# A bit field of the weight decode moves to a PSUM bank, and short-lived results share two banks instead of three

## The chip, the cores and the metric

The kernel runs on one core of a Trainium2 chip. The core has five engines that run side by side: TensorE (PE in the profile; PEld is its loading of stationary weights), VectorE (DVE), ScalarE (ACT), GpSimd (POOL) and SyncE (SP), which only issues transfers here. Results of TensorE land in PSUM[...]; everything else lives in SBUF. The metric is the device time of one execution in microseconds (us). The kernel before took 1086.1 us (median of three runs, 1086.04 to 1087.46).

## What is computed

Two blocks follow each other: an attention in which a query sees only the keys of its own cluster, and a feed-forward block with a hard-swish gate.

```python
# B, H, S, D = 4, 8, 768, 64; 16 clusters per head
q_assign = argmax(normalised(q) @ normalised(centroids))      # per head
k_assign = argmax(normalised(k) @ normalised(centroids))
mask   = q_assign[:, :, :, None] == k_assign[:, :, None, :]
scores = where(mask, q @ k.T / 8, -1e9)
attn   = softmax(scores) @ v                                   # (B, H, S, D)
x = attn.transpose(0, 2, 1, 3).reshape(3072, 512)
h = x @ w_in                                                   # w_in: 512 x 2048
y = (h * clip(h + 3, 0, 6) / 6) @ w_out                        # w_out: 2048 x 512
```

The weights `w_in` and `w_out` arrive as 64-bit floats. [...]the kernel takes each weight as two 32-bit words (`lo`, `hi`) and builds the 32-bit float from them: this is the *decode*, in 32 chunks of 128 x 512 weights.

## The kernel before

The work goes in rounds of two score tiles (`n`, `n + 1`); twelve tiles make a pair of heads, 48 a batch. The decode is spread over the first two batches (`n` = 0 to 94), so that it lies beside the attention. From `n` = 54 on the feed-forward block of the first batch (`ph`) is mixed in as well.

PSUM's eight banks are used like this: scores `ps` four (two tiles of two banks), `pv` one, the pool `psum_t` one, the pool `psum_m` two.

```python
psum_s = pool("psum_s", 2, space=PSUM)
psum_v = pool("psum_v", 1, space=PSUM)
psum_t = pool("psum_t", 1, space=PSUM)
psum_m = pool("psum_m", 2, space=PSUM)
...
st = {"scratch": 0}

def scratch(shape, name):          # the short-lived results pqk, pcs, pr, po, pd
    st["scratch"] += 1
    if st["early"] and st["scratch"] % 3:
        return psum_m.tile(shape, F32, name=name, tag="m")
    return psum_t.tile(shape, F32, name=name, tag="t")
```

While `st["early"]` holds, that is until the decode ends, two of three short-lived results go to `psum_m` and one to `psum_t`. The feed-forward results `ph` and `py` always go to `psum_m`.

The decode of a chunk is five steps; three to five of them (once one) are emitted at the end of each round:

```python
def split():
    load_weights(i + 1)                       # transfer of the next chunk, two buffers
    raw = st.pop(("raw", i))
    got.update(lo=raw[:, :, 0], hi=raw[:, :, 1])
    got["size"] = decp.tile([P, WC], BF16, name="wsize")
    got["top"]  = decp.tile([P, WC], U32, name="wtop")      # SBUF
    got["unit"] = decp.tile([P, WC], U32, name="wunit")     # SBUF
    nc.scalar.activation(out=got["size"], in_=hi, func=ACT.Abs, ...)
    nc.vector.tensor_scalar(out=top, in0=hi, ...)           # L219: hi << 3, masked
def join():
    nc.vector.scalar_tensor_tensor(out=top, in0=hi, in1=top, ...)   # L225
def power():
    nc.scalar.activation(out=got["size"], in_=got["size"], func=ACT.Relu, ...)
    nc.vector.tensor_scalar(out=unit, in0=top, ...)         # L235: & 0xFF800000
def rest():
    nc.vector.scalar_tensor_tensor(out=unit, in0=lo, in1=unit, ...) # L241
def total():
    nc.vector.tensor_tensor(out=weight, in0=top, in1=unit, op=ALU.add)  # L246
# (arguments cut)
```

The parts of the attention that matter here, per round and in the order in which they are emitted:

```python
scores(n)        # PE: ps <- xf (L371), += xm (L371); ACT: ex = exp(ps) (L383);
                 # POOL: acc += ex (L387, L390)
attn_v(n - 2)    # PE: pv += v * ex (L400)
later            # ACT: range sums of the last rcp (L433, L434), or counts
divide           # every third round: PE: pd <- ones, acc (L421);
                 # DVE: rcp = 1 / pd (L425), xT = num * rcp (L426)
prep of the next pair, by place r of the round in its pair:
  r = 0, 2: turn: PE: pqk (L295), ACT: xf <- pqk (L297), twice per round
  r = 4: PE: pcs (L308), ACT: cs <- pcs (L313)
  r = 6: PE: pr (L319), DVE: mx, one_hot <- pr (L322, L328)
  r = 8: route_turn twice, r = 10: once: PE: po (L351), ACT: xm <- po (L355)
feed-forward: PE: ph (L457), ACT and DVE: g_sb <- ph (L444, L445)
decode steps: share = {0: 5, 2: 3, 4: 4, 6: 1, 8: 3, 10: 4}
```

`divide` falls on the rounds with r = 2 and r = 8, so a `pd` is always followed by two `pqk` or two `po` (with a `ph` ahead of the first one in some rounds).

Of the kernel before, what the change touches and what calls it, by code (L numbers as in the profile page):

```python
# [10 lines left out]
U32 = mybir.dt.uint32  # L11
# [7 lines left out]
P = 128  # L19
# [10 lines left out]
WC = 512  # L30
# [86 lines left out]
def fast_path(ctx, tc, ok, q, k, v, centroids, moe_w_in, moe_w_out, out):  # L117
# [6 lines left out]
    def pool(name, bufs, **kw):  # L124
        return ctx.enter_context(tc.tile_pool(name=name, bufs=bufs, **kw))
# [14 lines left out]
    decp = decoding.enter_context(tc.tile_pool(name="decp", bufs=2))  # L140
# [3 lines that stand above are left out]
# [17 lines left out]
    counts = const.tile([P, 2, NPAIR], F32, name="counts")  # L161
    w_low = const.tile([P, 1], F32, name="w_low")

    st = {"scratch": 0}
    later = []

    def scratch(shape, name):

        st["scratch"] += 1
        if st["early"] and st["scratch"] % 3:  # L170
            return psum_m.tile(shape, F32, name=name, tag="m")
        return psum_t.tile(shape, F32, name=name, tag="t")

# [25 lines left out]
    def load_weights(i):  # L199
        if i < len(chunks):  # L200
            st["raw", i] = rawp.tile([P, WC, 2], U32, name="raw")
            nc.sync.dma_start(st["raw", i], chunks[i][1])

    def decoding_steps(i):

        got = {}

        def split():
            load_weights(i + 1)
            raw = st.pop(("raw", i))  # L210
            got.update(lo=raw[:, :, 0], hi=raw[:, :, 1])
            got["size"] = decp.tile([P, WC], BF16, name="wsize")
            got["top"] = decp.tile([P, WC], U32, name="wtop")
            got["unit"] = decp.tile([P, WC], U32, name="wunit")
            nc.scalar.activation(
                out=got["size"], in_=got["hi"].bitcast(F32), func=ACT.Abs,
                accum_out=w_totals[:, 0, i : i + 1],
            )
            nc.vector.tensor_scalar(  # L219
                out=got["top"], in0=got["hi"], scalar1=3, scalar2=0x3FFFFFFF,  # L220
                op0=ALU.logical_shift_left, op1=ALU.bitwise_and,
            )

        def join():
            nc.vector.scalar_tensor_tensor(  # L225
                out=got["top"], in0=got["hi"], scalar=0xC0000000, in1=got["top"],
                op0=ALU.bitwise_and, op1=ALU.bitwise_or,
            )

        def power():  # L230
            nc.scalar.activation(
                out=got["size"], in_=got["size"], func=ACT.Relu, bias=w_low, scale=-1.0,
                accum_out=w_totals[:, 1, i : i + 1],
            )
            nc.vector.tensor_scalar(  # L235
                out=got["unit"], in0=got["top"], scalar1=0xFF800000, scalar2=None, op0=ALU.bitwise_and
            )

        def rest():
            unit = got["unit"].bitcast(F32)  # L240
            nc.vector.scalar_tensor_tensor(  # L241
                out=unit, in0=got["lo"], scalar=2.0**-52, in1=unit, op0=ALU.mult, op1=ALU.mult
            )

        def total():
            nc.vector.tensor_tensor(  # L246
                out=chunks[i][0], in0=got["top"].bitcast(F32), in1=got["unit"].bitcast(F32), op=ALU.add
            )

        return [split, join, power, rest, total]  # L250


# [19 lines left out]
    def centroid_norm():  # L272
        cn = unit_rows(nc, smallp, cen, D)

        nc.scalar.activation(out=w_totals[:, 0, 0:1], in_=w_low, func=ACT.Exp)

        wide = smallp.tile([P, 2, D], F32, name="cenwide")
        for t in range(2):
            nc.vector.tensor_scalar_mul(out=wide[:, t], in0=cn, scalar1=parity[:, t : t + 1])
        pc = scratch([P, P], "pc")  # L280
        nc.tensor.transpose(out=pc, in_=wide, identity=ident)
        nc.vector.tensor_copy(out=cnT, in_=pc)
# [5 lines left out]
    def turn(g, part):  # L288
        if part == 0:
            st["xf", g] = xp.tile([P, NC2, P], F32, name="xf")  # L290
        qk, xf = st["qk", g], st["xf", g]
        pt = scratch([P, NHC, P], "pqk")
        for i in range(NHC):
            j = part * NHC + i
            nc.tensor.transpose(out=pt[:, i], in_=qk[:, j // NCH, j % NCH], identity=ident)  # L295
        dst = xf[:, part * NHC : (part + 1) * NHC]
        nc.scalar.copy(out=dst, in_=pt)  # L297
        if part == 3:
            st.pop(("qk", g))
# [4 lines left out]
    def cluster_scores(g):  # L304
        c0, xf = (2 * g) % H * C, st["xf", g]
        ps = scratch([P, 512], "pcs")[:, 0 : NC2 // 4 * P]
        for a in range(4):
            nc.tensor.matmul(  # L308
                ps[a * 2 * C : (a + 1) * 2 * C], lhsT=cnT[:, c0 : c0 + 2 * C], rhs=xf[:, a::4],
                start=True, stop=True,  # L310
            )
        cs = st["cs", g] = rtp.tile([P, NC2 // 4, P], F32, name="cs")
        nc.scalar.copy(out=cs, in_=ps)  # L313
# [707 lines left out]
@with_exitstack  # L1021
def kernel(
    ctx: ExitStack,
    tc: tile.TileContext,
    q: bass.AP,
    k: bass.AP,
    v: bass.AP,
    centroids: bass.AP,
    moe_w_in: bass.AP,
    moe_w_out: bass.AP,  # L1030
    out: bass.AP,
):
    ins = (q, k, v, centroids, moe_w_in, moe_w_out)
    flagp = ctx.enter_context(tc.tile_pool(name="flagp", bufs=1))
    ok = flagp.tile([1, 1], I32, name="ok")
    with ExitStack() as inner:
        fast_path(inner, tc, ok, *ins, out)
    with tc.If(tc.nc.values_load(ok[0:1, 0:1], min_val=0, max_val=1) == 0):
        with ExitStack() as inner:
            general_path(inner, tc, *ins, out)  # L1040
# [32 lines left out]
```

## Time and profile before

| | busy us | share of the span | instructions |
|---|---|---|---|
| PE | 1044.8 | 96% | 5218 |
| PEld | 673.4 | 62% | 5218 |
| DVE | 429.6 | 40% | 609 |
| ACT | 395.3 | 36% | 798 |
| POOL | 303.3 | 28% | 171 |

The profiled execution has a span of 1085.0 us. A group row of the profile reads: line, engine, operation, output and inputs, shape and count, then busy time and the mean of one in ns, then the idle time of the engine ahead of these instructions and who ended it. In the timeline a row is start, duration, engine, line, operation; in brackets stands the idle time before it and who ended it. A row of windows is a stretch of time with the busy time of each engine in it and the clock granted to TensorE. The decode's first VectorE record starts at 15.2 us, its last at 284.9 us.

### The profile page before, as it was taken

How to read it: one execution, taken by the hardware profiler on the slowest of the kernel's cores; microseconds unless marked ns; L12 is line 12 of the kernel's file. 1: busy time of each engine (PE TensorE's matmuls, PEld its weight loads, DVE VectorE, ACT ScalarE, POOL GpSimd, SP SyncE). 2: the span in 40 equal slices, each digit the busy share in tenths (PEclk: the TensorE clock that was granted, in tenths of full speed). 3: DMA queues.
4: the chain of work that ended last, by engine and by line, in shares of the span. 5: the costliest groups of instructions: out<-in, count | busy, mean ns of one | idle time of the engine just before them, and what ended most of it. 6: DMA issues, size and time to landing. Idle time of an engine off the chain costs nothing.

```text
span 1085.0 us, 12781 instructions
## 1 busy us (share of the span) xinstructions
PE 1044.8 (96%) x5218; PEld 673.4 (62%) x5218; DVE 429.6 (40%) x609; ACT 395.3 (36%) x798; POOL 303.3 (28%) x171
## 2 busy tenths in 40 slices
PE   6988889999999999999999999999999999999997
PEld 3433344444445544776677667676667678888886
DVE  5888897678312202421331321332232141413141
ACT  6777666666301301333432442432242330102010
POOL 3756565464310101323231322322322320000000
PEclk9989899999999999999999999999999999999999
DMA  5444442434002000020200202020100000000000
GB/s 146 95 106 111 102 111 70 102 86 119 1 19 54 1 10 20 1 44 21 44 1 1 63 1 44 21 44 1 34 1 1 20 1 1 21 20 1 20 1 24
DMA packets 83540, 42.89 MB, mean 40 GB/s; under 512 B 76304, under 2 KB 76304, under 8 KB 83472
## 3 DMA queue, kind: packets, MB, share of 16 engines
q1 hardware_dynamic: 83328, 41.95, 15.1%
q8 instruction: 43, 0.70, 0.3%
q14 instruction: 25, 0.20, 0.1%
q10 hardware_dynamic: 144, 0.03, 0.0%
HBM read 35.68 MB, written 6.29 MB: 39 GB/s over the span
## 4 chain that ended last, share of the span: by engine, by line
PE 88%; DVE 7%; ACT 2%; issue 1%; DMA 1%; POOL 0%; DVEq 0%; POOLq 0%; ACTq 0%; SPq 0%
PE ph L521 24%; PE ps L371 13%; PE Y L539 12%; PE pv L400 10%; PE X L539 9%; PE py L474 8%; PE ph L457 7%; DVE rcp L425 2%; PE pd L421 2%; PE pqk L295 2%; DVE w_in_sb L246 1%; DVE wunit L241 1%; DVE wtop L219 1%; PE pcs L308 1%; PE po L351 1%
## 5 line engine op out<-in xcount | busy, mean ns | idle before, releaser
L390 POOL TENSOR_TENSOR acc<-acc,ex 128x768 f32<-128x768 f32 x128 | 240.9, 1882 | 399.3 <-ACT ex L383 394.3
L521 PE MATMUL ph<-xT,w_in_sb 128*128 128x256 f32 x1152 | 259.6, 382 | 0.0
L521 PEld LDWEIGHTS ph<-xT,w_in_sb 128*128 128x128 f32 x1152 | 215.3, 190 | 46.2 <-issue 18.1
L383 ACT ACTIVATE ex<-ps 128x768 f32<-128x768 f32 x192 | 150.2, 807 | 139.5 <-PE ps L371 139.0
L444 ACT ACTIVATE g_sb<-ph,half_c 128x512 f32<-128x512 f32 (+1 forms) x104 | 68.1, 654 | 313.6 <-PE ph L521 245.8
L445 DVE SCALAR_TENSOR_TENSOR g_sb<-g_sb,ph 128x512 f32<-128x512 f32 (+1 forms) x104 | 67.2, 646 | 279.6 <-ACT g_sb L444 279.5
L371 PE MATMUL ps<-xf 64*128 64x384 f32 x768 | 170.2, 522 | 4.2 <-ACT ex L383 4.2
L400 PE MATMUL pv<-ex,vt 128*64 128x384 f32 x768 | 146.1, 502 | 0.0
L425 DVE RECIPROCAL rcp<-pd 128x384 f32<-128x384 f32 x32 | 81.8, 2555 | 81.2 <-PE pd L421 81.2
L387 POOL TENSOR_TENSOR acc<-ex 128x768 f32<-128x768 f32 x32 | 60.2, 1883 | 183.9 <-ACT ex L383 183.6
L400 PEld LDWEIGHTS pv<-ex,vt 128*64 128x64 f32 x768 | 46.9, 137 | 81.8 <-issue 77.1
L371 PEld LDWEIGHTS ps<-xf 64*128 64x128 f32 x768 | 64.9, 191 | 52.2 <-issue 30.9
L457 PE MATMUL ph<-xT,w_in_sb 128*128 128x384 f32 x256 | 87.3, 493 | 1.6 <-DVE rcp L425 1.6
L474 PE MATMUL py<-w_out_sb,g_sb 128*128 128x512 f32 x192 | 84.0, 594 | 0.0
L457 PEld LDWEIGHTS ph<-xT,w_in_sb 128*128 128x128 f32 x256 | 47.2, 190 | 41.1 <-issue 6.7
L539 PE MATMUL Y<-w_out_sb,g_sb 128*128 128x256 f32 x288 | 66.1, 383 | 0.0
L546 DVE TENSOR_TENSOR y<-y,Y 128x256 f32<-128x256 f32 x36 | 15.1, 420 | 127.2 <-PE Y L539 126.6
L539 PE MATMUL Y<-T,g_sb 128*128 128x256 f32 x288 | 65.3, 380 | 0.0
L539 PE MATMUL X<-w_out_sb,g_sb 128*128 128x256 f32 x288 | 65.3, 380 | 0.0
L371 PE MATMUL ps<-xm 64*128 64x384 bf16 x384 | 64.4, 330 | 0.3 <-ACT xm L355 0.3
L474 PEld LDWEIGHTS py<-w_out_sb,g_sb 128*128 128x128 f32 x192 | 35.9, 190 | 44.2 <-issue 43.3
L539 PEld LDWEIGHTS Y<-w_out_sb,g_sb 128*128 128x128 f32 x288 | 53.9, 190 | 12.9 <-issue 6.0
(88 smaller groups left out, 833.9 us busy)
## 6 DMA issues: line engine op xcount, KB each, us to landing
raw<-in_moe_w_in_dram SPq DMA_DIRECT2D x16, 512.0 KB, 3.7
raw<-in_moe_w_out_dram SPq DMA_DIRECT2D x16, 512.0 KB, 3.6
qk<-in_q_dram SPq DMA_DIRECT2D x32, 192.0 KB, 4.1
qk<-in_k_dram SPq DMA_DIRECT2D x32, 192.0 KB, 4.2
vt<-in_v_dram SPq DMA_DIRECT2D x32, 192.0 KB, 4.2
out_dram<-y SPq DMA_DIRECT2D x24, 256.0 KB, 2.1
cen<-in_centroids_dram ACTq DMA_DIRECT2D x1, 32.0 KB, 1.7
```

The source lines that it names most:

```text
L371: nc.tensor.matmul(st["ps", n][:, t, 0:HALF], lhsT=x[r, NCH + j], rhs=x[r, hf * NHC : (hf + 1) * NHC], start=first, stop=not first,)
L383: nc.scalar.activation(out=ex, in_=sc, func=ACT.Exp, scale=SM_SCALE)
L387: nc.gpsimd.tensor_tensor(out=acc, in0=st["ex", n - 1], in1=ex, op=ALU.add)
L390: nc.gpsimd.tensor_tensor(out=acc, in0=acc, in1=ex, op=ALU.add)
L400: nc.tensor.matmul(pv[t * D : (t + 1) * D], lhsT=vt[:, j, t], rhs=ex[:, t], start=(j == 0), stop=(j == NCH - 1),)
L425: nc.vector.reciprocal(out=rcp, in_=pd)
L444: nc.scalar.activation(out=g, in_=h, func=ACT.Relu, bias=half_c, scale=1.0 / 6.0)
L445: nc.vector.scalar_tensor_tensor(out=g, in0=g, scalar=1.0, in1=h, op0=ALU.min, op1=ALU.mult)
L457: nc.tensor.matmul(hh, lhsT=w_in_sb[:, kt, f * P : (f + 1) * P], rhs=xT[:, kt, hf * HALF : (hf + 1) * HALF], start=(kt == 0), stop=(kt == ...
L474: nc.tensor.matmul(py, lhsT=st["g", f][:, i * P : (i + 1) * P], rhs=w_out_sb[:, f], start=(f == 0), stop=(f == NFT - 1),)
L521: nc.tensor.matmul(ph[:, t * HC : (t + 1) * HC], lhsT=w_in_sb[:, kt, f * P : (f + 1) * P], rhs=xT[:, kt, 2 * m * P : 2 * (m + 1) * P], sta ...
L539: nc.tensor.matmul(bank[:, half * HC : (half + 1) * HC], lhsT=g_sb[:, kind, i], rhs=w[:, i], start=(first and i == 0), stop=(last and i == ...
```

## The change

The decode's intermediate `wtop` (sign and leading bits of a chunk's weights) moves from SBUF to the single bank of `psum_t`. In exchange the short-lived results no longer use that bank until the decode ends: all of them go to the two banks of `psum_m`, in turn, with `ph` from the second batch on. Once the decode has ended, everything is as before. The change is for the VectorE steps of the decode: four of the five now have `wtop` as an operand in PSUM.

```diff
-    st = {"scratch": 0}
+    st = {}
     later = []

     def scratch(shape, name):

-        st["scratch"] += 1
-        if st["early"] and st["scratch"] % 3:
+        if st["early"]:
             return psum_m.tile(shape, F32, name=name, tag="m")
         return psum_t.tile(shape, F32, name=name, tag="t")
@@
             got["size"] = decp.tile([P, WC], BF16, name="wsize")
-            got["top"] = decp.tile([P, WC], U32, name="wtop")
+            got["top"] = psum_t.tile([P, WC], U32, name="wtop", tag="t")
             got["unit"] = decp.tile([P, WC], U32, name="wunit")
```

## The prediction

> **What bounds the kernel now.** I read the page's strip of 40 slices first, then windows for stages, then the chain of waits, then VectorE's groups, then the timeline.
>
> ```profile
> PE   6988889999999999999999999999999999999997
> DVE  5888897678312202421331321332232141413141
> PEclk9989899999999999999999999999999999999999
> PE 88%; DVE 7%; ACT 2%; issue 1%; DMA 1%; POOL 0%; DVEq 0%; POOLq 0%; ACTq 0%; SPq 0%
> ```
>
> PE is TensorE, DVE VectorE, ACT ScalarE, POOL GpSimd. From slice 8 on TensorE is full; only slices 0 to 7 (some 200 us) have gaps, a lower clock and a full VectorE. The change acts only until the decode ends, at 285 us, so I split that stretch:
>
> ```profile
> 34.00:153.00 119.00, 101.63 (x629) 44.56 (x625) 105.38 (x96) 82.49 (x184) 75.91 (x39) 0.93 0.37 97
> 164.00:217.00 53.00, 50.78 (x279) 24.87 (x280) 36.63 (x47) 34.88 (x78) 24.55 (x13) 1.00 0.31 83
> 217.00:285.00 68.00, 68.00 (x376) 32.67 (x372) 50.09 (x62) 46.34 (x103) 36.88 (x19) 1.00 0.34 82
> ```
>
> The columns are the stretch, its length, the busy time of PE, PEld, DVE, ACT and POOL, and then the granted clock. Stage 1 (34 to 153 us: the end of the first pair's first `divide` to the first `ph`) has TensorE idle for 119 - 101.6 = 17.4 us and at clock 0.93, another 0.07 x 119 = 8.3 us: **25.7 us lost**. VectorE is busy 105.4 of 119. Stage 2 (153 to 285 us) loses little: its gaps in the timeline are 0.61, 0.91, 0.92 and 0.71 us, 3.2 in all, and TensorE is its bound. Everything later is full of TensorE work that the change leaves alone, so what stages 1 and 2 gain or lose should reach the end one for one.
>
> What takes VectorE's time in stage 1 (groups of VectorE, 15 to 152 us; busy time, mean ns):
>
> ```profile
> L246 DVE TENSOR_TENSOR w_in_sb<-wtop,wunit 128x512 f32<-128x512 f32 x16 | 23.4, 1461 | 0.5
> L219 DVE TENSOR_SCALAR wtop<-raw 128x512 uint32<-128x512 uint32 x17 | 21.6, 1272 | 2.1 <-DMA raw<-in_moe_w_in_dram 2.1
> L241 DVE SCALAR_TENSOR_TENSOR wunit<-raw,wunit 128x512 f32<-128x512 uint32 x17 | 18.2, 1072 | 0.4
> L225 DVE SCALAR_TENSOR_TENSOR wtop<-raw,wtop 128x512 uint32<-128x512 uint32 x17 | 14.8, 869 | 0.6
> L235 DVE TENSOR_SCALAR wunit<-wtop 128x512 uint32<-128x512 uint32 x17 | 10.1, 596 | 0.4
> ```
>
> These sum to 5.27 us per chunk. Their shortest records over the whole run are 412, 677, 417, 681 and 691 ns (L219, 225, 235, 241, 246), 2.88 us together. So 2.4 us of each chunk is not work. The timeline shows what it is:
>
> ```profile
> 46.17 4.03 POOL L390 TENSOR_TENSOR acc<-acc,ex 128x768 f32<-128x768 f32 x2 [2.20 <-ACT ex L383]
> 46.21 2.32 DVE L246 TENSOR_TENSOR w_in_sb<-wtop,wunit 128x512 f32<-128x512 f32 x1
> 48.45 2.03 DVE L219 TENSOR_SCALAR wtop<-raw 128x512 uint32<-128x512 uint32 x1
> ...
> 54.67 2.54 DVE L425 RECIPROCAL rcp<-pd 128x384 f32<-128x384 f32 x1
> 57.32 0.56 DVE L426 TENSOR_TENSOR xT<-num,rcp 128x384 f32<-128x384 f32 x1
> ...
> 57.91 0.52 ACT L433 ACTIVATE rcp<-rcp 128x384 f32<-128x384 f32 x1 [4.96 <-DVE xT L426]
> ...
> 59.68 0.90 PE L319 MATMUL pr<-ident,cs 128*128 128x128 f32 x3 [4.05 <-ACT cs L313]
> ```
>
> A decode step that starts beside a GpSimd addition takes 2.0 to 2.3 us. The `pd` of this round was done at 46.6, but its reciprocal came at 54.67: VectorE was 8 us behind. ScalarE[...] waited 4.96 us for `xT`, and TensorE 4.05 us for ScalarE's copy. After such a gap the scores ran at half speed (one round of them took 3.57 us in the chain at 61 us, 1.82 elsewhere). That is the loss of stage 1.
>
> [...]L445, which reads one SBUF and one PSUM operand, spans only 540 to 690 ns over two sizes, and the reciprocal out of PSUM 2544 to 2559, while each decode step reaches 2.0 to 2.3 us.
> [...]412 ns for L219 against 691 ns for the copy of `py` out of PSUM, at 512 elements each.
> [...]
>
> **The change part by part.**
> (a) `wtop` in PSUM. L219 writes PSUM and L235 reads it[...] and go to about 0.69 us (from the 691 ns copy), +0.55 us per chunk. In return L219, L225, L235 and L246 have at most one SBUF operand[...]. GpSimd does 10 additions of 1.85 us per 26 us, a share of 0.71, so L241 should wait 0.71 x 0.93 = 0.65 us on average. Per chunk: 5 x 0.69 + 0.65 = 4.1 us instead of 5.27: **1.2 us less per chunk**, 17 chunks in stage 1: 20 us of 105. VectorE's load per pair of heads (12 rounds, four chunks) becomes 4 x 4.1 + 2 x 2.6 (reciprocals) + 2 x 0.8 (`xT`) + 1.25 (routing) + gaps = about 25.
>
> (b) Is that enough? TensorE's own work per pair at full clock, from undisturbed rows: six rounds of two score tiles and their `pv`, 1.82 + 1.44 each, is 19.6; two `pd` 1.3, four `pqk` 1.4, `pcs` 0.8, `pr` 0.5, `po` 0.9: 24.5 us. Stage 1 is 3.8 pairs, 93.7 us, against 119 measured (which gives the 25 lost again). VectorE and TensorE would now be nearly level, so VectorE's lag falls from 8 us to 1 or 2, which the next round covers: ScalarE should no longer be held up.
>
> (c) Two banks instead of three for `pqk`, `pcs`, `pr`, `po` and `pd`. I first took strict rotation; then each `pd` would block the second block after it until the reciprocal ends, 2.3 us, some ten times. The program as built shows otherwise: beside a `pd` the next two blocks (`po`,`po` or `pqk`,`pqk`) share the other bank, and the second waits for ScalarE's copy of the first. Two such places exist now, and give the price:
>
> ```profile
> 201.28 0.27 PE L351 MATMUL po<-ident_q,one_hot 128*128 128x128 bf16 x2 [0.92 <-ACT xm L355]
> 215.00 0.55 PE L295 MATMUL pqk<-ident,qk 128*128 128x128 f32 x3 [0.71 <-ACT xf L297]
> ```
>
> So about 0.8 us each. Counting in the built order: 8 new ones in stage 1 (6.4 us) and 8 in stage 2 (6.4 us), and about 0.5 us at the start.
>
> (d) Sum. Stage 1: 93.7 + 6.4 and some 4 for what VectorE's and ScalarE's queues still collide = 104, against 119: **-15**. Stage 2: +6.4, less 1.5 for gaps that came from VectorE's lag (0.61 and 0.91): **+5**. Start +0.5. Together about -9.5: 1086.1 - 9.5 = 1076.5 us.
>
> **The rivals.**
> - [...]If the second block waits for the reciprocal after all, or ScalarE is busy with an exponential (0.80 us) when a copy is due, each of 16 places costs 2 us or more: stages 1 and 2 lose 32 and the result is 1086 to 1095. For it: stage 2 is full of TensorE, nothing there hides a stall. Against: in the two places shown ScalarE was idle before its copy.
> - *VectorE stays the bound.* If L241 inherits a whole addition each time (its longest record is 2.3 us), a chunk costs 5.1 us and stage 1 gains next to nothing: with the +5 of stage 2, 1088 to 1091. Against: GpSimd idles 0.29 of the time, and L241's mean is only 1.07 us now.
> - *A transfer takes the wait's place.* `raw` needs 3.7 us to land, and a chunk's transfer starts when the chunk before last is freed; the six VectorE steps in between take some 4.8 us in the new kernel. It fits, with 1 us to spare; if not, a few us of stage 1 are lost.
> - *Everything is recovered.* All 25.7 us of stage 1 less 6.4, and stage 2 at +5: 1072; without any new bank wait 1057 (29 us less), which I hold for out of reach.
>
> **Range and chances.** The total of loss that could be recovered is 29 us, the new bank waits cost some 13, so a gain over 2% (21.7 us) needs those waits to be hidden: 0.03. A loss over 2% needs more than 27 places that cost 0.8 us without any gain: 0.02. Range 1069 to 1086: the upper end is a stage 1 that gains 6, the lower one a stage 1 that gains 20 with cheaper stalls.
>
> **What would show it.** Step (a): L219 and L235 near 0.69 us with almost no spread, L225 and L246 too, L241 alone with records of 2 us; VectorE's busy time down by some 20 us. Step (b): the first `ph` at about 138 us instead of 153; the waits of ScalarE for `xT` (18.2 us) nearly gone, the clock in slices 0 to 7 near full. Step (c): new waits of TensorE for the copies of `xf` and `xm`, 0.7 to 0.9 us each, some 16 more; from the first `ph` to the end of the decode some 137 us instead of 132. The prediction is wrong if these waits are for the reciprocal, if L241 grows past 1.6 us, or if what follows the decode changes its length.

## The result, and the profile after

The changed kernel takes 1074.2 us (median of four runs) against 1086.8 us of the kernel before on the same chip: a ratio of 0.9877, with a 95% interval of 0.9851 to 0.9903. It is 12.6 us faster. The profiled executions, which the stages below are read from, span 1071.3 and 1085.0 us.

The page of the changed kernel (its line numbers are lower by one: L218 is the old L219, L240 the old L241):

```profile
PE   6999999999999999999999999999999999999997
DVE  5788855565122103420331331332241232314141
PEclk9999999999999999999999999999999999999999
PE 96%; ACT 2%; DVE 1%; issue 0%; POOL 0%; POOLq 0%; DVEq 0%
```

TensorE is full from the second slice on, its clock has no dip any more in the 40 slices, and VectorE's share of the chain that ended last has fallen from 7% to 1%. The two stages of the decode as windows (length, then busy time of PE, PEld, DVE, ACT and POOL, then the clock):

```profile
33.00:134.00 101.00, 96.03 (x630) 42.63 (x627) 86.68 (x104) 85.85 (x193) 71.94 (x40) 1.00 0.45 117
134.00:271.00 137.00, 129.77 (x694) 62.28 (x695) 80.21 (x112) 86.00 (x190) 63.64 (x35) 1.00 0.34 83
```

Stage 1 (end of the first pair's first `pd` to the first `ph`) has shrunk from 119 to 101 us, at full clock. Stage 2 (first `ph` to the end of the decode) has grown from 132 to 137 us, and TensorE now idles 7 us in it. VectorE's groups from 15 to 152 us:

```profile
L240 DVE SCALAR_TENSOR_TENSOR wunit<-raw,wunit 128x512 f32<-128x512 uint32 x20 | 18.7, 936 | 0.5
L224 DVE SCALAR_TENSOR_TENSOR wtop<-raw,wtop 128x512 uint32<-128x512 uint32 x20 | 14.0, 700 | 0.7
L218 DVE TENSOR_SCALAR wtop<-raw 128x512 uint32<-128x512 uint32 x20 | 13.9, 695 | 2.5 <-DMA raw<-in_moe_w_in_dram 2.0
L234 DVE TENSOR_SCALAR wunit<-wtop 128x512 uint32<-128x512 uint32 x20 | 13.8, 688 | 0.5
L245 DVE TENSOR_TENSOR w_in_sb<-wtop,wunit 128x512 f32<-128x512 f32 x16 | 11.1, 691 | 0.6
```

The four steps with `wtop` in PSUM take 0.69 to 0.70 us on average, and none of their records up to 290 us is longer than 0.72. Of the five steps only L240, which has two SBUF inputs, has a mean above that. TensorE's own waits from 20 to 290 us:

```profile
PE pqk L294 <- ACT xf L296: 6.2, 10, 0.7
PE po L350 <- ACT xm L354: 6.0, 8, 0.9
PE ps L370 <- ACT ex L382: 0.3, 1, 0.3
```

The columns are the total in us, how often, and the longest. The 18 waits for ScalarE's copies, 12.2 us in all, are what can be seen of the price of the two banks; two of them, 0.9 and 0.7 us, were there before. ScalarE's waits for `xT`, 18.2 us in the kernel before, are gone from its own list.

### The profile page after: what moved, and what is told of

It reads as the page before. It is cut to its first block, busy times and chain, and to the rows that moved or that the text cites. A ratio compares the mean times of both kernels' runs of the same rounds, so it can differ in the third digit from the quotient of the medians.

```text
span 1071.3 us, 12812 instructions
## 1 busy us (share of the span) xinstructions
PE 1038.9 (97%) x5218; PEld 669.9 (63%) x5218; DVE 391.5 (37%) x609; ACT 395.9 (37%) x798; POOL 295.3 (28%) x171
## 4 chain that ended last, share of the span: by engine, by line
PE 96%; ACT 2%; DVE 1%; issue 0%; POOL 0%; POOLq 0%; DVEq 0%
PE ph L520 24%; PE ps L370 16%; PE pv L399 13%; PE Y L538 12%; PE X L538 9%; PE ph L456 8%; PE py L473 8%; PE pqk L294 2%; PE pd L420 2%; PE pcs L307 1%; PE po L350 1%; ACT g_sb L443 1%; ACT xm L354 1%; PE pr L318 1%; ACT xf L296 1%
## 5 line engine op out<-in xcount | busy, mean ns | idle before, releaser
L389 POOL TENSOR_TENSOR acc<-acc,ex 128x768 f32<-128x768 f32 x128 | 235.2, 1837 | 410.0 <-ACT ex L382 404.9
L370 PE MATMUL ps<-xf 64*128 64x384 f32 x768 | 165.5, 509 | 0.3 <-ACT ex L382 0.3
L386 POOL TENSOR_TENSOR acc<-ex 128x768 f32<-128x768 f32 x32 | 58.0, 1813 | 167.5 <-ACT ex L382 167.5
```

The costliest lines, as they stand in the source:

```text
L370: nc.tensor.matmul(st["ps", n][:, t, 0:HALF], lhsT=x[r, NCH + j], rhs=x[r, hf * NHC : (hf + 1) * NHC], start=first, stop=not first,)
L386: nc.gpsimd.tensor_tensor(out=acc, in0=st["ex", n - 1], in1=ex, op=ALU.add)
L389: nc.gpsimd.tensor_tensor(out=acc, in0=acc, in1=ex, op=ALU.add)
```

## The experiments

All kernels of this study. The time is the median; the ratio is to runs of the kernel before on the same chip (medians 1086 to 1087). The other columns are in us and split one profiled execution of each at the same two events, first `ph` and first `py` (the latter starts less than 1 us from the end of the last decode step):

| kernel | time, us | ratio to before, 95% | first `ph` at | `ph` to `py` | `py` to the end |
|---|---|---|---|---|---|
| before | 1086.8 | | 153.1 | 132.1 | 799.8 |
| changed | 1074.2 | 0.9851 to 0.9903 | 133.8 | 137.6 | 799.9 |
| banks only | 1091.9 | 1.0035 to 1.0068 | 150.3 | 139.1 | 800.0 |
| before, without additions | 1060.9 | 0.9748 to 0.9781 | 127.5 | 130.4 | 800.8 |
| changed, without additions | 1075.6 | 0.9882 to 0.9916 | 134.7 | 137.7 | 800.7 |
| `wunit` in PSUM | 1073.9 | 0.9870 to 0.9903 | 134.1 | 137.7 | 799.8 |
| reorder | 1071.0 | 0.9836 to 0.9865 | 140.7 | 130.6 | 799.5 |
| reorder in stage 2 | 1066.5 | 0.9803 to 0.9830 | 134.6 | 130.3 | 799.7 |
| reorder, without additions | 1063.7 | 0.9778 to 0.9808 | 130.7 | 130.6 | 800.5 |
| reorder, `rcp` in PSUM | 1063.3 | 0.9776 to 0.9802 | 131.8 | 130.7 | 799.4 |

The last column stays within 1.4 us: what the decode's stages win or lose reaches the end nearly one for one.

**1. The banks alone.** `wtop` goes back to SBUF, the new use of the banks stays.

```diff
-            got["top"] = psum_t.tile([P, WC], U32, name="wtop", tag="t")
+            got["top"] = decp.tile([P, WC], U32, name="wtop")
```

> The bank part alone: wtop stays in SBUF, the short-lived results go to two banks in turn, the third bank is empty until the decode ends. [...]the decode steps keep their records of 2.0 to 2.3 us, stage 1 stays as long as in the kernel before or a little longer (first ph at 150 to 158 us), stage 2 takes some 137 us as in the changed kernel: 1088 to 1096 us. Rival (the new order of banks itself helps, because a pd no longer blocks a pcs or pqk that follows it in the rotation): 1074 to 1080 us with the long decode steps still there.

Measured: 1091.9 us, slower than before. Its VectorE groups from 15 to 152 us, and the timeline:

```profile
L224 DVE SCALAR_TENSOR_TENSOR wtop<-raw,wtop 128x512 uint32<-128x512 uint32 x18 | 24.4, 1358 | 0.6
L245 DVE TENSOR_TENSOR w_in_sb<-wtop,wunit 128x512 f32<-128x512 f32 x16 | 17.1, 1068 | 0.6
L240 DVE SCALAR_TENSOR_TENSOR wunit<-raw,wunit 128x512 f32<-128x512 uint32 x17 | 11.7, 691 | 0.4
```

```profile
55.70 0.52 ACT L432 ACTIVATE rcp<-rcp 128x384 f32<-128x384 f32 x1 [4.03 <-DVE xT L425]
57.47 0.72 PE L318 MATMUL pr<-ident,cs 128*128 128x128 f32 x3 [2.27 <-ACT cs L312]
```

The long steps are still there, spread over other steps than before (in this stretch L240 has none, L224 most), and so is the chain of waits from `xT` over ScalarE to TensorE. The bank part costs 7.0 us in stage 2 and gives back 2.8 us up to the first `ph`, 1.2 of them ahead of the first `pd`. So the gain comes from `wtop` in PSUM (1074.2 against 1091.9 us), and the banks are what it costs.

**2 and 3. GpSimd's additions taken out.** In the kernel before and in the changed one, the same edit; the softmax sums of the first two batches are then incomplete, all other work is there.

```diff
             acc = st["acc", g, hf]
-            nc.gpsimd.tensor_tensor(out=acc, in0=acc, in1=ex, op=ALU.add)
+            if not st["early"]:
+                nc.gpsimd.tensor_tensor(out=acc, in0=acc, in1=ex, op=ALU.add)
```

> The kernel before (wtop in SBUF, three banks), but GpSimd's additions of the third to sixth exponential tile are left out until the decode ends, so the softmax sums of the first two batches are incomplete; everything else is as before. [...]a chunk takes 2.9 to 3.1 us, TensorE is the bound of stage 1 (first ph at 128 to 133 us), stage 2 stays at 130 to 132 us: 1060 to 1066 us. Rival (VectorE's work as such, the landing of raw, or ScalarE's queue bounds stage 1): 1076 us or more, with steps at their short times.

> The changed kernel, with the same additions left out until the decode ends. [...]TensorE with its bank waits already bounds both stages; its mean falls from 0.84 to 0.69 us and the time stays within 2 us of the changed kernel: 1072 to 1075 us, slower than the kernel before without the additions, which has three banks. Rival[...]: 5 us or more less than the changed kernel.

Measured: the kernel before gains 25.9 us (1060.9), the changed kernel nothing (1075.6, just above the range expected). The mean in the second expectation is that of L240 up to the end of the decode: 843 ns in the changed kernel, and records of 684 to 693 ns without the additions. VectorE has the same work in both versions of the kernel before; only the other engine's additions are gone, and its step L246 falls from 1461 to 692 ns:

```profile
L246 DVE TENSOR_TENSOR w_in_sb<-wtop,wunit 128x512 f32<-128x512 f32 x16 | 11.1, 692 | 0.5
```

A chunk still took 3.3 us here, not the expected 2.9 to 3.1: seven steps (four L219, three L225) are long, up to 2.35 us, and each of them overlaps a first addition of an accumulator (`acc<-ex`), which the edit had left in. In the kernel before, TensorE, VectorE and ScalarE never waited for GpSimd from 15 to 290 us, so the additions cost nothing as a result that came late. So the loss of stage 1 was the meeting of the two engines, not VectorE's work, the transfer of `raw` or ScalarE. In the changed kernel that loss is gone already, and without the additions it is the slower one of the two by 14.7 us: 7.2 up to the first `ph` and 7.3 after it, the price of the two banks. The new waits of TensorE account for 10.6 us of this; 0.6 us lie ahead of the first `pd`, and where the rest arises was not traced.

**4. The other intermediate in PSUM.**

```diff
-            got["top"] = psum_t.tile([P, WC], U32, name="wtop", tag="t")
-            got["unit"] = decp.tile([P, WC], U32, name="wunit")
+            got["top"] = decp.tile([P, WC], U32, name="wtop")
+            got["unit"] = psum_t.tile([P, WC], U32, name="wunit", tag="t")
```

> The changed kernel with the other intermediate in the PSUM bank: wunit in PSUM, wtop in SBUF. [...]the shift is back at 0.42 us when free, [...]a chunk costs 3.8 to 4.3 us, below what TensorE needs per pair; the time is that of the changed kernel, 1073 to 1077 us, with records of 2 us on L218 and L224 alone. Rival[...]: 1078 us or more.

Measured: 1073.9 us, the same as the changed kernel. Of the decode's steps from 15 to 152 us two are long on average, the shift L218 (SBUF to SBUF) and the join L224 (two SBUF inputs); L240 stands beside them for comparison:

```profile
L224 DVE SCALAR_TENSOR_TENSOR wtop<-raw,wtop 128x512 uint32<-128x512 uint32 x20 | 22.8, 1142 | 0.7
L218 DVE TENSOR_SCALAR wtop<-raw 128x512 uint32<-128x512 uint32 x20 | 18.4, 919 | 1.3 <-DMA raw<-in_moe_w_in_dram 1.3
L240 DVE SCALAR_TENSOR_TENSOR wunit<-raw,wunit 128x512 f32<-128x512 uint32 x20 | 13.9, 697 | 0.5
```

The records above 1 us are now on these two (up to 1.98 and 2.25 us), the steps without a PSUM operand; the other three stay at 0.68 to 0.72. So the step held up changed with the operand in PSUM: L240 in the changed kernel (up to 1.39 us), L218 and L224 here. A chunk costs VectorE 4.2 us here and 3.7 in the changed kernel, and the time is the same: VectorE does not bound either.

**5. The bank waits hidden.** In a round with two short blocks the first is emitted ahead of `pd` and `ph`, so that its copy runs beside them.

```diff
             m = n - lag_d + 1
+            prep = prep_items(g + 1, r)
+            if prep and (r == 4 or st["early"] and len(prep) == 2):
+                prep.pop(0)()
             if m >= 0 and m % NCH == NCH - 1:
                 later.append(divide(m))
-            prep = prep_items(g + 1, r)
-            if r == 4 and prep:
-                prep.pop()()
```

> The changed kernel with one order changed until the decode ends: in a round with two short blocks (two pqk or two po) the first is emitted ahead of pd and ph, the second stays behind them. So the copy of the first block runs beside pd (0.67 us) or ph (2.2 us), and the second block, which has the same bank, finds it free. Theory (the changed kernel is held by TensorE's work and by these bank waits, 0.57 to 0.9 us each, some 18 in all): in stage 1 a pair takes 25.0 us instead of 26.2, in stage 2 most of the waits go: 9 to 10 us less than the changed kernel, 1063 to 1067 us. Rival (VectorE or ScalarE stands right behind TensorE, and takes over as the bound, or the ph now waits for a reciprocal or a gate instead): 1070 us or more.

Measured: 1071.0 us, where 1063 to 1067 were expected. The interval of its ratio overlaps that of the changed kernel. Stage 2 did what was expected (130.6 us instead of 137.6), but the first `ph` came 6.9 us later: the first `pd` at 34.7 instead of 32.6, and then 27.4 to 28.3 us per pair instead of 26.2. VectorE's groups from 34 to 138 us and the timeline show why a pair takes longer:

```profile
L240 DVE SCALAR_TENSOR_TENSOR wunit<-raw,wunit 128x512 f32<-128x512 uint32 x15 | 22.5, 1502 | 0.4
L425 DVE TENSOR_TENSOR xT<-num,rcp 128x384 f32<-128x384 f32 x8 | 11.8, 1476 | 1.2 <-DVE rcp L424 0.5
```

```profile
66.37 3.90 POOL L389 TENSOR_TENSOR acc<-acc,ex 128x768 f32<-128x768 f32 x2 [0.67 <-ACT ex L382]
66.60 2.00 DVE L425 TENSOR_TENSOR xT<-num,rcp 128x384 f32<-128x384 f32 x1
68.52 2.30 DVE L240 SCALAR_TENSOR_TENSOR wunit<-raw,wunit 128x512 f32<-128x512 uint32 x1
68.64 0.52 ACT L432 ACTIVATE rcp<-rcp 128x384 f32<-128x384 f32 x1 [1.70 <-DVE xT L425]
```

The two steps that still have two SBUF inputs, `xT` and L240, now fall on GpSimd's additions, one behind the other, and ScalarE waits for `xT` again. In the changed kernel all 15 records of `xT` up to 290 us took 0.56 us. One of them, at 49.53 us, lies in a gap between two additions (one ended at 49.06, the next began at 50.79). TensorE pays for the longer `xT` at the `pqk` behind a `pd`, four times up to 133 us:

```profile
50.54 0.55 PE L294 MATMUL pqk<-ident,qk 128*128 128x128 f32 x3 [2.13 <-ACT xf L296]
```

**6 to 8. What stage 1 lost there.** One kernel keeps the reorder to the rounds with `ph` (the condition becomes `READY <= n < DECODED`), one takes GpSimd's additions out of the reordered kernel, to tell them from the order as the cause of its longer pairs, and one keeps the reciprocal of stage 1 in PSUM, so that `xT` too has a PSUM operand:

```diff
-        rcp = nump.tile([P, HALF], F32, name="rcp")
+        rcp = pd if n < per_batch else nump.tile([P, HALF], F32, name="rcp")
         nc.vector.reciprocal(out=rcp, in_=pd)
```

> The changed kernel with the order of the last run (first short block ahead of pd and ph) only where the feed-forward block is mixed in, n from 52 to 95. Theory: the last run gained 7 us between the first ph and the end of the decode (130.6 against 137.6 us) and lost the same in stage 1 (first ph at 140.7 against 133.8 us), because there xT and the step that reads raw and wunit began to meet GpSimd's additions. Then this kernel has the good half of each: first ph at 133 to 135 us, 130 to 132 us from there to the end of the decode, 1065 to 1068 us. Rival (the loss of stage 1 only moves[...]): 1070 us or more.

> The kernel of the last run (first short block ahead of pd and ph throughout), with GpSimd's additions of the third to sixth exponential tile left out until the decode ends, so the softmax sums of the first two batches are incomplete. [...]a pair takes 24.8 to 25.2 us without the additions, the first ph comes at 127 to 130 us: 1058 to 1062 us, level with the kernel before without the additions. If it came from the order itself[...], a pair keeps some 27 us and the time 1069 us or more.

> The kernel of the reorder throughout, and until n = 51 the reciprocal stays in PSUM, written over pd, so that xT reads one SBUF and one PSUM operand[...]; the range sums read it there as well. [...]xT is back at 0.56 us each time; [...]VectorE's lag shrinks, a pair of stage 1 takes 25 to 26 us and the first ph comes at 128 to 134 us: 1061 to 1067 us. Rival[...]: 1069 us or more, with records of 2 us there.

The records of 2 us in the last rival are those of L240. Measured: 1066.5, 1063.7 and 1063.3 us. The first has the good half of both kernels, as expected. The second takes 25.1 to 25.2 us from one `pd` to its like in the next pair, inside the expected 24.8 to 25.2, though its time and first `ph` came some 2 and 1 us later than expected. So it was GpSimd's additions that had lengthened a pair to 27.4 to 28.3 us, beyond the 26.2 us of the changed kernel, not the order. A pair of the kernel before without the additions is shorter still, 24.5 to 24.6 us; neither kernel has a wait of TensorE in this stage, and the 0.6 us between them stay open. The third keeps all of GpSimd's additions and reaches 25.1 to 25.2 us per pair from its second pair on:

```profile
63.79 4.05 POOL L389 TENSOR_TENSOR acc<-acc,ex 128x768 f32<-128x768 f32 x2 [0.66 <-ACT ex L382]
64.03 0.56 DVE L425 TENSOR_TENSOR xT<-num,pd 128x384 f32<-128x384 f32 x1
64.50 1.66 DVE L240 SCALAR_TENSOR_TENSOR wunit<-raw,wunit 128x512 f32<-128x512 uint32 x1
64.62 0.47 ACT L432 ACTIVATE pd<-pd 128x384 f32<-128x384 f32 x1 [0.26 <-DVE xT L425]
```

`xT` now runs beside an addition and takes 0.56 us; L240, right behind it, is still held up (1.66 us, against 0.69 without the additions), but TensorE has only one wait left up to the end of the decode, of 0.6 us. This kernel computes all of the reference, and at 1063.3 us (ratio 0.9789, 0.9776 to 0.9802) it is some 10 us faster than the changed one.

## Why the prediction was right, and where its terms were off

The prediction said 1076.5 us, 1069 to 1086; measured were 1074.2.

- *Step (a), the steps of the decode: right in kind, the wait of L240 sized too high.* That a step with `wtop` in PSUM would no longer be held up was the author's assumption; in the changed kernel L218 and L234 went to 0.69 us, L224 and L245 lost their spread (0.69 to 0.72 us). L240 waits 0.25 us on average from 15 to 152 us (936 less 691 ns) instead of the estimated 0.65. The term that failed is the assumption that L240 meets GpSimd at a random moment. In the changed kernel its long records come back once per pair, 26.2 us apart: 66.48, 92.69 and 118.89 us with 1.18 to 1.19 us, 77.99, 104.19 and 130.40 with 1.37 to 1.39. Over the same stretch the line has a mean of 691 ns in the banks-only kernel, 936 in the changed one and 1367 in the reordered one. The wrong size did not matter: without the additions L240 falls to 690 ns, and the changed kernel gets no faster. The prediction also left out that `xT` has two SBUF inputs, as L240 has, and counted it at the old 0.8 us. That it ran free in the changed kernel, at 0.56, was luck as far as the prediction goes; the reordered kernel shows what it costs when it does not. VectorE's busy time fell by 38 us over the run (429.6 to 391.5), not some 20, which counted stage 1 alone.
- *Step (b), TensorE becomes the bound of stage 1: right.* A pair takes 26.2 us (`pd` at 32.6, 58.8, 85.0, 111.2). Its own work was estimated at 24.5, and the kernel before without the additions takes 24.5 to 24.6; two bank waits of 0.67 and 0.57 come on top, and some 0.4 us are in no wait. Stage 1 gained 18 us instead of 15: its eight bank waits took 5.0 us instead of 6.4, and the 4 us put aside for collisions of VectorE's and ScalarE's queues were not used up. The first `ph` came at 133.8, not 138.
- *Step (c), the bank waits: right.* There were 18 waits of 0.68 us on average, where 16 new and two old ones of 0.8 were counted; stage 2 took 137.6 us, predicted 137. The wait is for ScalarE's copy, never for the reciprocal. Experiments 1 and 6 show the price from both sides: 7 us in stage 2.
- *The start:* +0.5 us was expected. The first `pd` came 1.2 us earlier than before (32.6 against 33.8); TensorE's clock from 16 to 25 us was 0.86 in the profile of before and full in the other. The kernel with the reorder in stage 2 alone is the changed kernel up to there and has its first `pd` at 33.4, also at full clock, so the same order of instructions differs by 0.8 us between two kernels. Whether the change has a part in the 1.2 us stays open.
- *The rivals:* the banks did not outweigh what `wtop` in PSUM gave (stage 1 became 18 us shorter, stage 2 5.5 us longer), VectorE did not stay the bound, and VectorE waited for `raw` no longer than before (2.0 against 2.1 us, once). A kernel without the new bank waits was held for out of reach at 1057 us; with another order of the blocks and `rcp` in PSUM it came to 1063.3.

## What to carry to other kernels

When VectorE and GpSimd work side by side, list the VectorE instructions whose records are longer beside GpSimd's (here decode steps of 0.42 to 0.69 us that took 2.0 to 2.3), find the ones that another engine waits for, and give these a PSUM operand first: it brought L246 from 1461 to 691 ns on average, and `xT` of the reordered kernel from 1.48 to 0.56 us. Holding up the others cost no time in experiments 4 and 8. It is not free in general: in the kernel before, long decode steps that no other engine waited for put VectorE 8 us behind, and with it the reciprocal and `xT`, for which ScalarE waited. So add up what VectorE has to do per pair as well. A PSUM bank taken for this is paid by those who shared it, with 7 us in stage 2 here: look in the built program for two short blocks in a row in one bank, and put other TensorE work between them. Where a step meets the other engine changed with the order of the program, so after each reordering read the durations again.

## What I had not expected of the hardware

- What VectorE loses to GpSimd's additions is a matter of phase. Moving one short block ahead of `pd` turned `xT` from 0.56 us each time into a mean of 1.48 us in stage 1, and a pair from 26.2 into 27.4 to 28.3 us, which took back most of the 7 us that stage 2 had won.
- The join reads and writes PSUM in place, in 32-bit integer form, and cost hardly more than its SBUF counterpart: it took 0.70 us with `wtop` in PSUM, against 0.69 for its free records in SBUF (512 elements). The shift took 0.69 us with PSUM as its output, against 0.42 free in SBUF.
- TensorE's clock stayed at 1.00 through stage 1 of the reordered kernel despite waits of 1.4 to 2.1 us, while the kernel before lost clock around waits of 3.2 to 5.0 us (0.50 from 60 to 66 and from 120 to 123 us, 0.68 from 95 to 98). But the banks-only kernel lost it as well, around waits of 2.3 us (ended at 57.47, 89.70 and 120.83 us) that were each followed by one of 0.7 to 0.8 us:

```profile
58.00:64.00 6.00, 5.34 (x19) 2.24 (x20) 3.60 (x7) 4.84 (x13) 3.87 (x3) 0.50 0.93 210
92.00:95.00 3.00, 3.00 (x13) 1.14 (x12) 1.85 (x4) 2.47 (x7) 2.92 (x2) 0.50 1.12 285
123.00:126.00 3.00, 3.00 (x12) 1.11 (x10) 1.98 (x5) 2.18 (x5) 2.82 (x2) 0.50 1.10 290
```

So waits of 2.3 us came with half the clock in one kernel, and waits of up to 2.1 us with the full clock in another; these runs give no length of wait that is safe.
